# Attention steps on TensorE moved within their slots, and output-weight conversions queued behind a later Silu

## The chip, the cores and the metric

The kernel runs on one core of a Trainium2 chip. The metric is the device time of one execution in microseconds (us); a lower time is better. Chunks, blocks and slots are counted from 0 throughout.

## The reference, cut to what matters

```python
def reference(q, k, v, moe, moe2):               # q, k, v: [4, 8, 576, 64] f32
    s = q @ k.T / 8                              # per batch and head
    s = where(mask, s, -1e9)                     # heads 0-3: the last 32 keys; heads 4-7: every 32nd key
    a = exp(s - max(s)); a = a / (sum(a) + 1e-9)
    x = heads_side_by_side(a @ v)                # [2304, 512]
    xn = x / sqrt(mean(x * x) + 1e-6) * moe.rms_g
    g = xn @ moe.w_gate                          # [2304, 1536]
    y = (g / (1 + exp(-g)) * (xn @ moe.w_val)) @ moe.w_out
    return ((y @ moe2.w_a) * (y @ moe2.w_b)) @ moe2.w_out
```

## The kernel before, in words

The 2304 tokens are cut into six blocks `t` of 384. The first stage runs attention and the first expert (gate, value, output) block by block; the second stage (from some 540 us on) does the second expert and is not touched by the change. Every product is made of three matmuls, with the operands split into a rounded high part and the rest (`mm3`).

Block `t` loops over twelve chunks `fc` of 128 hidden columns. For a chunk TensorE makes `g_ps` and `v_ps` (`mm_in`, lines 485 to 488, 24 matmuls of 384 columns), VectorE scales `g_ps` by the inverse norm `rinv` into `sg` (L774), ScalarE takes the Silu of `sg` (L776), VectorE multiplies by `v_ps` (L787), ScalarE casts the result to the high part of `hl` (L506, in `split`), VectorE or GpSimd subtracts for the low part (L507), and TensorE adds the chunk into `y` (`emit_y`, 12 matmuls, one chunk behind). `g_ps` and `v_ps` share three PSUM buffers.

Woven into the chunks of block `t` is the attention of block `t + 1`. `attention_slot(steps, fc)` traces the steps of slot `fc`, after the Silu of chunk `fc` and ahead of `emit_y` of chunk `fc - 1`. The local heads' steps are placed by the strings `LOCAL` (one for block 0, one for the later blocks, slots parted by `|`): loads `ll`, `lvl`; scores `qk` on TensorE, masked on VectorE (`smask`), row maximum `lmax`, `lexp` on ScalarE, `lnorm`; transposes `pt` on TensorE (L358), copied out by ScalarE (`ptc`, L368); `pv` on TensorE (L378) and its evacuation `pvc`. The strided heads are done with products on GpSimd and sums on VectorE; at their end `xst` (L412) transposes on TensorE and `xstc` evacuates. `rms` (L444) and `rinv` (L448, L450) close a block's attention. All of the attention's TensorE results of blocks 1 to 5 go through one PSUM buffer, `att`, so `qk`, `pt`, `pv`, `xst` follow one another only after each one's evacuation. In block 0 the exponentials are grouped (`exps`): they stand behind the Silu traced last, and the next Silu stands behind them.

In block 0 the weights are converted too. Each chunk's gate and value weights (`convert1`) and output weights pass ScalarE (L137 in place, L142 into `cz`), VectorE (L145), ScalarE (L150) and a subtraction, nearly always on GpSimd (L151). `cz` has one buffer for output weights. The converted output weights `wo` are stored by SyncE's queue (L793) and read back in blocks 1 to 5 (L615). The raw output weights of chunks 8 and 9 and later of 10 and 11 share two buffers (`load_late`).

The program is traced in this order, but each engine's own order is written by a planner when the kernel is compiled (`schedule_with_timeline_sim=True`, line 1032): it goes by its own model of when an instruction has what it needs. On the chip an engine runs its list in that order. `behind(instructions)` (lines 497 to 502) tells the planner to put what is traced inside it behind the given instruction on that instruction's engine; with a Silu that is ScalarE's list alone. `gate(fc)` does the same with steps of the first block's attention.

Of the kernel before, what the change touches and what calls it, by code (L numbers as in the profile page):

```python
# [47 lines left out]
         "snorm sqr sqrt xhi",  # L48
         "rec sexp snorm sqrt xhi"]

LOCAL = [("ll0 qk0 smask0 lmax0|ll1 qk1|smask1 qk2 lmax1 smask2 lmax2||lexp0 lexp1 lexp2|"
# [3 lines left out]


STRIDED1 = ("lq ls0 ls1 sqk00 sqk01 sqk02|sqk10 sqk11 sqk12|lv0 ssub|lv1|sexp snorm|spv00 spv01 spv02|spv10 spv11|"
# [20 lines left out]
def fused_kernel(ctx: ExitStack, tc: tile.TileContext, qtl, ktl, vl, qs, ks, vs, cst, w1, w2, out):  # L78
# [7 lines left out]
    def engine(c):  # L86
        return {"P": nc.gpsimd, "D": nc.vector}[c]
# [29 lines left out]
    def load_pair(w, which, pool=None):  # L117
        if pool is None:
            t = gv_slot(U32, "gv_raw")
            if which[0][1] == 0:  # L120
                gvraw[which[0][0]] = t
            return [load_raw(w, fc, k, t[:, i]) for i, (fc, k) in enumerate(which)]
        return [load_raw(w, fc, k, raw_third(pool)) for fc, k in which]
# [46 lines left out]
    def run(steps):  # L170
        for f in steps:
            f()
# [312 lines left out]
    def mm_in(ps, w, sel, x):  # L485
        for cc in range(NCC):
            c = slice(cc * 128, (cc + 1) * 128)
            mm3(ps, w[:, sel, 0, c], w[:, sel, 1, c], x[cc][:, 0], x[cc][:, 1], cc == 0, cc == NCC - 1)

    def tmp(name):  # L490
        return act.tile([128, NTB], F32, tag="t", name=name, bufs=NTMP)

    made = []
    silu, silu_gate = [], []

    @contextmanager
    def behind(instructions):

        with ExitStack() as e:
            for i in instructions:  # L500
                e.enter_context(tc.issue_after(i))
            yield

    def split(h, lo_eng):
        hl = act.tile([128, 2, NTB], F32R, tag="hl", name="hl", bufs=3)
        made.append(nc.scalar.copy(hl[:, 0], h).ins)  # L506
        made.append(lo_eng.tensor_tensor(hl[:, 1], h, hl[:, 0].bitcast(F32), op=ALU.subtract).ins)  # L507
        return hl
# [26 lines left out]
    def load_units(n):  # L535
        for which in units[:n]:
            raw.update(zip(which, load_pair(w1, which)))
        del units[:n]

    def load_late(which):  # L540
        raw.update(zip(which, load_pair(w1, which, pool)))

    def convert1(fc):
        t = gv[fc] = gv_slot(F32R, "gv")
        two = [raw.pop((fc, k)) for k in range(2)]
        if fc in FUSEDW:
            both, ready = gvraw[fc], t.rearrange("p k a n -> p (k a) n")
            run(conversion(both.rearrange("p k a n -> p (k a) n"), ready, pool, engine(WLO[fc][0]), LOW[fc][0]))
        else:
            run(zipped(*(conversion(two[k], t[:, k], pool, engine(WLO[fc][k]), LOW[fc][k]) for k in range(2))))  # L550
# [30 lines left out]
    @contextmanager  # L581
    def gate(fc):

        with behind(silu[:1] if fc > 4 else []), ExitStack() as e:
            for key in GATES[min(fc, len(GATES) - 1)].split():
                e.enter_context(tc.issue_after(s0["st"][key].ins))
            yield
# [7 lines left out]
    def emit_y(t, fc):  # L595
        if fc == 0:
            for e in range(NCC):
                y[t, e] = psum.tile([128, 512], F32, tag=f"y{e}", name=f"y{e}")
        h = hl.pop((t, fc))
        w = wo.pop((t, fc))  # L600
        for e in range(NCC):
            c = slice(e * 128, (e + 1) * 128)
            mm3(y[t, e][:, :NTB], w[:, 0, c], w[:, 1, c], h[:, 0], h[:, 1], fc == 0, fc == NFC - 1)

    def evac_y(t):
        for e in range(NCC):
            if e % 2 == 0:
                both = act.tile([128, 2, NTB], F32, tag="x", name="ys", bufs=8)
            ys = both[:, e % 2]
            nc.vector.tensor_tensor(ys, y[t, e][:, :NTB], ri[t], op=ALU.mult)  # L610
            nc.sync.dma_start(x2d[t, e // 2][:, e % 2], ys)

    def load_wo(t, fc):
        wt = wo[t, fc] = wo_tile()
        nc.sync.dma_start(wt.rearrange("p a n -> p (a n)").bitcast(F32), wod[fc])  # L615


    local = [dict(enumerate(order.split("|"))) for order in LOCAL]
    strided1 = dict(enumerate(STRIDED1.split("|")))

    def attention_slot(steps, fc):
        st = steps["strided"]
        n_sl = 10
        if t == 0:
            part = strided1.get(fc, "").split()
        else:
            part = st[len(st) * fc // n_sl:len(st) * (fc + 1) // n_sl] if fc < n_sl else []
        part += local[min(t, 1)].get(fc, "").split()
        part += ["rms", "rinv"] * (fc == n_sl)
        for n in part:  # L630
            steps[n]()

    def exps(steps):

        def together(f, key):
            def g():
                with behind([silu[-1]]):
                    f()
                silu_gate.append(steps["st"][key].ins)
            return g  # L640

        for n in ("lexp0", "lexp1", "lexp2"):
            steps[n] = together(steps[n], "exp")
# [98 lines left out]
    for t in range(NB):  # L742
        if t == 1:
            apool.close()
            pool = apool.enter_context(tc.tile_pool(name="attn", bufs=1))
        if t == NB - 1:
            apool.close()
            cpool.close()
            pool = p2.enter_context(tc.tile_pool(name="forms", bufs=1, reuse_waits="tile"))
            early = [f for k in (4, 5, 0, 1, 2, 3) for f in convert_forms(k, k < 4)]  # L750
        nxt = attention(t + 1, pool, psum, itertools.cycle(["att"])) if t + 1 < NB else None
        if t == 0:
            exps(nxt)
        x = [xt[t, cc] for cc in range(NCC)]
        for fc in range(NFC):
            if t > 0 and fc == 0:
                load_wo(t, 0)
            g_ps = psum.tile([128, 512], F32, tag="gv", name="g_ps", bufs=3)
            mm_in(g_ps[:, :NTB], gv[fc], 0, x)
            v_ps = psum.tile([128, 512], F32, tag="gv", name="v_ps", bufs=3)  # L760
            mm_in(v_ps[:, :NTB], gv[fc], 1, x)
            if t == 0 and fc + 1 < NFC:
                with gate(fc + 1):
                    convert1(fc + 1)
                if fc + 2 == NFC:
                    load_late([(NFC - 2, 2), (NFC - 1, 2)])
            if t == NB - 1:
                slab[fc] = wgt.tile([128, 4 * DM], F32 if fc in (0, 1, 11) else F32R, tag="gv", name="slab", bufs=NFC)
                with behind(made):
                    run(early[len(early) * fc // NFC:len(early) * (fc + 1) // NFC])  # L770
                    for k in [k for k in x0 if k <= fc]:
                        run(x0.pop(k))
            sg = tmp("sg")
            nc.vector.tensor_tensor(sg, g_ps[:, :NTB], ri[t], op=ALU.mult)  # L774
            with behind(silu_gate):
                silu.append(nc.scalar.activation(sg, sg, AF.Silu).ins)  # L776
            silu_gate[:] = []
            if fc == 1 and t > 0:
                evac_y(t - 1)
            if nxt is not None:  # L780
                attention_slot(nxt, fc)
            if prev is not None:
                emit_y(*prev)
            if t > 0 and fc + 1 < NFC:
                load_wo(t, fc + 1)
            h = tmp("h") if t else v_ps[:, :NTB]
            made[:] = [nc.vector.tensor_tensor(h, sg, v_ps[:, :NTB], op=ALU.mult).ins]  # L787
            hl[t, fc] = split(h, engine(HLO0[fc] if t == 0 else HLO[t]))
            if t == 0:
                wt = wo[0, fc] = wo_tile()  # L790
                with gate(fc + 1), behind(silu[:1] if fc > 1 else []):
                    run(conversion(raw.pop((fc, 2)), wt, pool, engine(WLO[fc][2]), LOW[fc][2], True))
                nc.sync.dma_start(wod[fc], wt.rearrange("p a n -> p (a n)").bitcast(F32))  # L793
                if fc % 2 and units:
                    load_units(1)
            prev = (t, fc)
    emit_y(*prev)
    evac_y(NB - 1)
# [138 lines left out]
    steps = [(ps, g, p) for ps in (range(0, 3), range(3, 6)) for g in range(NB // 2) for p in ps]  # L937
# [99 lines left out]
```

## Time and profile before

| | |
|---|---|
| time, median of 3 runs (lowest, highest) | 965.81 us (964.63, 966.51) |
| the profiled execution: time, span of the trace | 967.4 us, 965.6 us |
| mean granted TensorE clock in the span | 0.985 |
| busy share of the span: TensorE matmuls, VectorE, ScalarE, GpSimd | 97%, 64%, 44%, 56% |
| block 0 with its attention and conversions | from 33 to some 133 us |

The 1.8 us between the profiled time and its span lie outside the first and last instruction. A busy time of TensorE counts overlapping matmuls, so the steps between starts, the waits and the granted clock tell more than the share does.

### The profile page before, as it was taken

What the parts mean: (1) busy time and instruction counts of PE and PEld (TensorE: products, weight loads), DVE (VectorE), ACT (ScalarE), POOL (GpSimd) and SP (SyncE); (2) the same over time, 40 slices, a digit from 0 to 9 for tenths busy, and PEclk for the clock granted to TensorE, in tenths of its full rate; (3) what the DMA queues carried; (4) which work ended last, traced back from release to release, by engine and by line L of the source; (5) the groups of instructions that cost most, each with busy time, mean ns of one, the idle gap of its engine ahead of it and who ended that gap; (6) DMA issues with size and microseconds to landing.
All of it is one profiled execution on the core that took longest, in us unless ns stands there. A gap on an engine that the chain in (4) does not pass through costs nothing.

```text
span 965.6 us, 14099 instructions
## 1 busy us (share of the span) xinstructions
PE 937.1 (97%) x5318; PEld 888.2 (92%) x5318; DVE 621.5 (64%) x900; ACT 425.3 (44%) x795; POOL 539.5 (56%) x407
## 2 busy tenths in 40 slices
PE   5998999999999999999999899999999999999998
PEld 4898999999999999999999898899999998999996
DVE  5658858658819895986666378658655655564534
ACT  5988646344433434434555455436425422122110
POOL 3567946558649677878479545655724423123211
PEclk6899999999999999999999999999999999999999
DMA  9974286537535563532788884996993974754701
GB/s 342 408 262 151 89 288 218 151 96 225 165 104 161 161 204 102 185 105 87 284 324 306 329 306 166 402 415 247 385 373 114 345 274 165 284 205 168 267 2 66
DMA packets 57363, 215.55 MB, mean 223 GB/s; under 512 B 5968, under 2 KB 14544, under 8 KB 51664
## 3 DMA queue, kind: packets, MB, share of 16 engines
q1 hardware_dynamic: 57296, 214.66, 61.3%
q8 instruction: 42, 0.69, 0.3%
q14 instruction: 25, 0.20, 0.1%
HBM read 172.17 MB, written 42.47 MB: 222 GB/s over the span
## 4 chain that ended last, share of the span: by engine, by line
PE 65%; DMA 11%; DVE 7%; POOL 7%; ACT 4%; issue 4%; SPq 0%; DVEq 0%; ACTq 0%; POOLq 0%
PE o L916 5%; PE o L918 5%; PE o L917 5%; DMA raw<-in_w 4%; POOL prod L248 4%; PE Y L862 4%; PE Y L861 4%; PE Y L860 4%; DMA gv_raw<-in_w 3%; PE y L482 3%; PE y L481 3%; PE g_ps L483 3%; PE y L483 3%; PE g_ps L482 3%; PE g_ps L481 3%
## 5 line engine op out<-in xcount | busy, mean ns | idle before, releaser
L151 POOL TENSOR_TENSOR hl<-c,hl 128x384 fp32r<-128x384 f32 x72 | 77.9, 1082 | 181.0 <-ACT hl L150 174.4
L248 POOL TENSOR_TENSOR prod<-kv_t,qs_t 128x512 f32<-128x512 f32 (+12 forms) x57 | 108.3, 1921 | 15.3 <-DMA kv_t<-in_ks 8.2
L481 PE MATMUL v_ps<-xx,gv 128*128 128x384 f32 x288 | 97.7, 339 | 1.9 <-DVE sg L774 1.8
L482 PE MATMUL y<-hl,wo 128*128 128x384 f32 x288 | 98.1, 341 | 1.1 <-POOL hl L507 1.1
L281 POOL TENSOR_TENSOR prod<-kv_t,S_t 128x512 f32<-128x512 f32 (+12 forms) x57 | 86.2, 1526 | 21.1 <-issue 7.1
L482 PE MATMUL v_ps<-xx,gv 128*128 128x384 f32 x288 | 97.9, 340 | 0.0
L483 PE MATMUL v_ps<-xx,gv 128*128 128x384 f32 x288 | 97.8, 340 | 0.0
L481 PE MATMUL g_ps<-xx,gv 128*128 128x384 f32 x288 | 97.5, 339 | 0.0
L483 PE MATMUL g_ps<-xx,gv 128*128 128x384 f32 x288 | 97.3, 338 | 0.0
L482 PE MATMUL g_ps<-xx,gv 128*128 128x384 f32 x288 | 96.9, 337 | 0.0
L867 DVE TENSOR_TENSOR c<-c,Y 128x384 f32<-128x384 f32 x108 | 59.0, 551 | 58.8 <-PE Y L862 53.5
L507 POOL TENSOR_TENSOR hl<-h,hl 128x384 fp32r<-128x384 f32 x60 | 64.1, 1069 | 58.4 <-ACT hl L506 57.3
L483 PE MATMUL y<-hl,wo 128*128 128x384 f32 x288 | 95.0, 338 | 0.0
L284 DVE TENSOR_REDUCE xs_t<-prod 128x64 f32<-128x448 f32 (+17 forms) x57 | 85.7, 1521 | 9.7 <-POOL prod L281 9.5
L481 PE MATMUL y<-hl,wo 128*128 128x384 f32 x288 | 85.0, 343 | 7.0 <-ACT hl L506 5.4
L916 PE MATMUL o<-slab,hl 128*128 128x512 f32 x216 | 84.7, 393 | 1.8 <-DVE slab L925 1.3
L917 PE MATMUL o<-slab,hl 128*128 128x512 f32 x216 | 84.5, 392 | 0.0
L918 PE MATMUL o<-slab,hl 128*128 128x512 f32 x216 | 83.2, 394 | 0.0
L150 ACT CAST hl<-c 128x384 fp32r<-128x384 f32 x72 | 37.0, 514 | 93.8 <-DVE c L897 93.5
L776 ACT ACTIVATE sg<-sg 128x384 f32<-128x384 f32 x72 | 38.0, 528 | 86.4 <-DVE sg L774 86.0
L862 PE MATMUL Y<-slab,form 128*128 128x384 f32 x216 | 73.0, 338 | 0.0
L861 PE MATMUL Y<-slab,form 128*128 128x384 f32 x216 | 73.0, 338 | 0.0
(137 smaller groups left out, 2491.4 us busy)
## 6 DMA issues: line engine op xcount, KB each, us to landing
form<-formd SPq DMA_DIRECT2D x32, 1792.0 KB, 10.7
wo<-wod SPq DMA_DIRECT2D x60, 512.0 KB, 3.8
raw<-in_w SPq DMA_DIRECT2D x40, 512.0 KB, 7.3
gv_raw<-in_w SPq DMA_DIRECT2D x32, 512.0 KB, 10.2
formd<-form SPq DMA_DIRECT2D x6, 1792.0 KB, 7.5
formd<-forms SPq DMA_DIRECT2D x6, 1792.0 KB, 12.8
slab<-x2d SPq DMA_DIRECT2D x24, 384.0 KB, 4.0
wod<-wo SPq DMA_DIRECT2D x12, 512.0 KB, 3.4
```

What stands on the lines that cost most here:

```text
L151: lo_eng.tensor_tensor(lo, x, hi.bitcast(F32), op=ALU.subtract)
L248: nc.gpsimd.tensor_tensor(pr, st["ks", g][:, :, :n, :], st["qs"][:, heads(g), mm:mm + 1, :].to_broadcast([128, G, n, D]), op=ALU.mult)
L281: st["pvm"] = nc.gpsimd.tensor_tensor(pr, st["vs", g][:, :, :n, :], st["S"][:, heads(g), mm, :n, None].to_broadcast([128, G, n, D]), op=AL ...
L284: st["pvr"] = nc.vector.tensor_reduce(st["xs"][:, mm, heads(g), :], pr.rearrange("p g n d -> p g d n"), axis=X, op=ALU.add)
L481: nc.tensor.matmul(out_ps, w_hi, x_hi, start=start, stop=False)
L482: nc.tensor.matmul(out_ps, w_hi, x_lo, start=False, stop=False)
L483: nc.tensor.matmul(out_ps, w_lo, x_hi, start=False, stop=stop)
L861: nc.tensor.matmul(bank(n), hi, x[p][:, 1, c], start=False, stop=False, skip_group_check=not begins)
L862: nc.tensor.matmul(bank(n), lo, x[p][:, 0, c], start=False, stop=c == 1, skip_group_check=not begins)
L916: nc.tensor.matmul(o, h[:, 0, cols], w[0], start=n == 0, stop=False)
L917: nc.tensor.matmul(o, h[:, 0, cols], w[1], start=False, stop=False)
L918: nc.tensor.matmul(o, h[:, 1, cols], w[0], start=False, stop=n == len(chunks) - 1)
```

## The change

Three things are done. The strings `LOCAL` place the local heads' steps anew: in block 0 `pt`, `pv` and their copies come later by up to one slot; in blocks 1 to 4 the local loads come a slot earlier, the three `lexp` stand together in slot 3, and `pt0` moves from slot 4 to 5. A `/` in a slot parts steps that are traced where the slot was from steps that are traced behind the chunk's `emit_y`, `split` and, in block 0, output-weight conversion; `xst1` and `xstc1` always go to that second place. And the output-weight conversion of chunk `n` (from 2 on) is put behind the Silu of chunk `n - 2`, where it stood behind the Silu of chunk 0.

```diff
-LOCAL = [("ll0 qk0 smask0 lmax0|ll1 qk1|smask1 qk2 lmax1 smask2 lmax2||lexp0 lexp1 lexp2|"
-          "lnorm0 lvl0 pt0 ptc0 lnorm1 lvl1|pt1 ptc1 lnorm2 pt2 ptc2|pv0 pvc0 pv1 pvc1||"),
-         ("|ll0 qk0|ll1 qk1 smask0 smask1 qk2 lmax0 lmax1|lvl0 smask2 lexp0 lmax2 lexp2|"
-          "lnorm0 lexp1 lvl1 pt0 ptc0 lnorm1 lnorm2|pt1 pt2 ptc1||ptc2 pv0 pvc0 pv1 pvc1||")]
+LOCAL = [("ll0 qk0 smask0 lmax0|ll1 qk1 smask1 lmax1|qk2 smask2 lmax2||lexp0 lexp1 lexp2|"
+          "lnorm0 lvl0 lnorm1 lvl1 lnorm2|pt0 ptc0/pt1 ptc1|pt2 ptc2|pv0 pvc0/pv1 pvc1||"),
+         ("ll0|qk0 smask0 lmax0 ll1|qk1 smask1 lmax1/qk2 smask2 lmax2|lexp0 lexp1 lexp2 lvl0|"
+          "lnorm0 lnorm1 lnorm2 lvl1|pt0 ptc0/pt1 ptc1|pt2 ptc2|pv0 pvc0/pv1 pvc1||")]
...
-    def attention_slot(steps, fc):
+    def attention_slot(steps, fc, late):
...
-        part += local[min(t, 1)].get(fc, "").split()
-        part += ["rms", "rinv"] * (fc == n_sl)
+        part = [n for n in part if (n in ("xst1", "xstc1")) == late]
+        early, _, behind_y = local[min(t, 1)].get(fc, "").partition("/")
+        part += (behind_y if late else early).split()
+        part += ["rms", "rinv"] * (fc == n_sl and not late)
...
             if nxt is not None:
-                attention_slot(nxt, fc)
+                attention_slot(nxt, fc, False)
             if prev is not None:
                 emit_y(*prev)
...
-                with gate(fc + 1), behind(silu[:1] if fc > 1 else []):
+                with gate(fc + 1), behind(silu[max(fc - 2, 0):max(fc - 1, 1)] if fc > 1 else []):
                     run(conversion(raw.pop((fc, 2)), wt, pool, engine(WLO[fc][2]), LOW[fc][2], True))
...
+            if nxt is not None:
+                attention_slot(nxt, fc, True)
             prev = (t, fc)
```

## Rows read from the trace of the kernel before

**Rows 1.** The page: an engine's busy us (share) and count; a load's KB, landing us.

```profile
PE 937.1 (97%) x5318; PEld 888.2 (92%) x5318; DVE 621.5 (64%) x900; ACT 425.3 (44%) x795; POOL 539.5 (56%) x407
...
wo<-wod SPq DMA_DIRECT2D x60, 512.0 KB, 3.8
```

**Rows 2.** Windows: stretch, length, busy PE, PEld, DVE, ACT, POOL, granted clock, DMA share.

```profile
33.00:60.00 27.00, 23.54 (x123) 21.97 (x122) 16.31 (x20) 26.67 (x40) 10.14 (x5) 0.94 1.03 408
60.00:86.00 26.00, 26.00 (x168) 25.61 (x166) 19.19 (x31) 20.47 (x51) 24.27 (x14) 1.00 0.37 124
86.00:96.00 10.00, 6.99 (x32) 5.84 (x31) 9.59 (x15) 9.45 (x17) 4.43 (x3) 0.83 0.57 197
96.00:133.00 37.00, 35.62 (x225) 34.07 (x225) 28.79 (x35) 25.94 (x43) 26.14 (x17) 1.00 0.38 133
...
134.00:540.00 406.00, 403.40 (x2467) 393.72 (x2466) 280.98 (x377) 177.63 (x341) 292.75 (x216) 1.00 0.57 190
```

**Rows 3.** TensorE's waits, 34 to 134 us: total us, times, longest.

```profile
PE y L481 <- ACT hl L506: 5.4, 3, 2.1
```

**Rows 4.** TensorE's timeline at chunk 0's output: start, us, instruction, idle time before it.

```profile
49.59 0.34 PE L483 MATMUL v_ps<-xx,gv 128*128 128x384 f32 x1
51.78 0.97 PE L481 MATMUL y<-hl,wo 128*128 128x384 f32 x4 [1.85 <-ACT hl L506]
```

**Rows 5.** The chain that ended last, from 51 us: start, us, what.

```profile
51.37 0.36 ACT hl L506
...
53.29 0.32 PE y L483
...
56.49 0.27 PE g_ps L483
...
57.10 0.18 PE g_ps L483
...
64.58 0.88 PE att L296 x8
```

**Rows 6.** ScalarE's timeline, 45 to 59 us.

```profile
45.09 0.67 ACT L137 ACTIVATE gv_raw<-gv_raw 128x512 f32<-128x512 f32 x1
...
46.20 2.80 ACT L137 ACTIVATE gv_raw<-gv_raw 128x512 f32<-128x512 f32 x4
48.87 0.55 ACT L776 ACTIVATE sg<-sg 128x384 f32<-128x384 f32 x1
...
51.23 0.50 ACT L506 CAST hl<-v_ps 128x384 fp32r<-128x384 f32 x1
...
53.14 1.30 ACT L137 ACTIVATE gv_raw<-gv_raw 128x512 f32<-128x512 f32 x2
...
58.21 0.73 ACT L137 ACTIVATE raw<-raw 128x512 f32<-128x512 f32 x1
```

**Rows 7.** VectorE's timeline: the scaled gate of chunk 1.

```profile
46.96 0.56 DVE L774 TENSOR_TENSOR sg<-g_ps,rinv 128x384 f32<-128x384 f32 x1
```

**Rows 8.** TensorE's timeline, 87 to 90 us.

```profile
87.01 0.61 PE L358 MATMUL att<-cst_sb,s_t 128*96 128x128 f32 x4 [0.71 <-ACT pt L368]
89.75 0.96 PE L481 MATMUL y<-hl,wo 128*128 128x384 f32 x4 [2.13 <-ACT hl L506]
```

**Rows 9.** Timelines at the end of block 0, on TensorE, ScalarE and VectorE.

```profile
119.03 0.27 PE L412 MATMUL att<-cst_sb,xs_t 128*128 128x128 f32 x1
...
123.54 0.67 ACT L137 ACTIVATE raw<-raw 128x512 f32<-128x512 f32 x1 [0.40 <-DMA raw<-in_w]
...
124.37 0.81 PE L444 MATMUL att<-sq,ones 128*128 128x384 f32 x2
...
128.09 0.58 ACT L448 ACTIVATE rms_t<-att,eps_sb 128x384 f32<-128x384 f32 x1
...
128.71 2.55 DVE L450 RECIPROCAL rinv<-rms_t 128x384 f32<-128x384 f32 x1 [0.74 <-ACT rms_t L448]
...
132.83 0.96 PE L481 MATMUL y<-hl,wo 128*128 128x384 f32 x4 [1.39 <-ACT hl L506]
```

## The prediction

> **What bounds the kernel now.** I read the page's busy shares first [rows 1]: TensorE is at 97%, no other engine over 64%, so a change that adds or drops no matmul can win only where TensorE waits or runs at its lower clock. The table of windows then says where that is [rows 2]. From 134 to 540 us, which are blocks 1 to 5, TensorE is busy 403.40 of 406 at a clock of 1.00: at most 2.6 us lie there for the taking. From 60 to 86 it is busy throughout. What is left stands in block 0: 3.46 idle us from 33 to 60 (clock 0.94), 3.01 from 86 to 96 (clock 0.83) and 1.38 from 96 to 133. The view of waits gives most of it one name: in that block TensorE waited three times, 5.4 us in all, for ScalarE's cast of `hl` [rows 3]. The three waits are 1.85 at 51.78 [rows 4], 2.13 at 89.75 [rows 8] and 1.39 at 132.83 [rows 9].
>
> The first one is where the third edit strikes. `hl` of chunk 0 is cast at 51.23, behind the Silu of chunk 1 at 48.87, and straight ahead of that Silu stand four L137 [rows 6]; ScalarE is busy 26.67 of 27 us in this stretch [rows 2]. Three of the four have the form of output weights, by the order of the loads those of chunks 3, 4 and 5; the fourth prepares a chunk's gate and value weights. Nobody needs the three soon: the matmuls that read them are three chunks and more away. The chain that ended last goes through just this cast: from `hl` at 51.37 to TensorE, which then runs without a wait until the first scores at 64.58 [rows 5], and over VectorE and GpSimd to the end of block 0. So a cast that comes earlier is worth something beyond its own gap. TensorE's clock falls right behind the wait: the matmuls from 53.29 to 56.49 advance by 0.32 us each, those from 57.10 on by 0.18 [rows 5]. That is 1.2 GHz against 2.4 GHz, after TensorE had been idle for 1.85 us.
>
> **The change, part by part.** The sum is made against the profiled execution (967.4 us, span 965.6, 1.8 outside it); it lies 1.6 us over the median of 965.81, and I take the gain off that median.
>
> *Conversions behind Silu n-2.* The edit acts on ScalarE's list alone. The steps of chunk n that stand ahead of Silu n-2 today are L137: three ahead of Silu 1 at 48.87, two at 53.14 (chunks 6 and 7) and two up to 58.21 (chunks 8 and 9) [rows 6]. Their later steps need the one `cz` buffer and come behind their Silu already. One L137 of this form takes 0.67 and, overlapping the next, moves the list on by about 0.56 (at 46.20 four, one of them of the double form, take 2.80) [rows 6]. Without three of them Silu 1 could start 1.68 earlier, at 47.19; but its input is ready at 47.52 [rows 7], so it starts at about 47.57 and the gain is 1.30. The cast moves from 51.23 to 49.93, and `y`, which started 0.55 behind it, to 50.48. TensorE is free at 49.93 [rows 4]. The wait of 1.85 becomes 0.55: **1.30 us gained**. Bounds: 0, if the planner puts other ready work in the freed places, or L137 of chunk 3, free behind Silu 1, ahead of the cast together with it; 1.85, if the cast is planned before the gate weights that stand between it and Silu 1.
>
> *The clock behind that wait.* Eleven matmuls, from the one at 53.29 to the one at 56.49, at 0.32 instead of 0.18 cost 11 x 0.14, some **1.55 us** [rows 5]. With the idle time cut to less than a third I take the fall as gone; bounds 0 and 1.55. The Trainium skill, "TensorE: Matmul & The Clock Gate", section "Seeing it yourself", warns that the clock events of a trace have been seen to be unreliable. If the fall were a fault of the record, this term would be nothing and the forecast 964.9. The start steps of 0.32 and 0.18 are not clock events, and they show the fall as well, so I keep the term.
>
> *The L137 that move.* Those of chunks 3 to 6 go to places between 48.87 and some 66, ScalarE has 5.5 idle us from 60 to 86 [rows 2]: nothing. Those of chunks 7 to 9 now stand behind Silu 5, 6 and 7. The cast of chunk 5, which can't come before Silu 5, is the one that TensorE waits for until 89.75 [rows 8], so these three land in the stretch from 86 to 96, where ScalarE is busy 9.45 of 10 [rows 2]. Ahead of that cast they would cost up to 1.68; they are traced later than it and I take 0. VectorE's, GpSimd's and SyncE's steps of the conversions follow; the stores of `wo` are first read back at the start of block 1, and a load of it lands after 3.8 us [rows 1].
>
> *`pt1`, `pt2` behind `y`.* TensorE now does `pt1` at 87.01 inside its hole, after 0.71 of waiting for the copy of `pt0`, and then waits for the cast of chunk 5 until 89.75 [rows 8]. Behind `y` of chunk 5 the hole goes from 86.3 to 89.75 as before, since the cast of chunk 5 is what ends it, and the four transposes come on top: a loss of **0.4** (0.61 as the row has them, less their overlap with what follows; bounds 0 and 0.61). The stall that the edit is meant for isn't removed, it changes its name.
>
> *`pv1`, `xst1`, `xstc1` later.* They are all links of one chain over the single `att` buffer. `xst1` ends today at 119.03, when its last input comes, the sum of squares is added up by 124.37, and the root of it follows only at 128.09, behind other work on ScalarE [rows 9]: between the end of that matmul (125.2) and the root lie some 2.9 us in which the chain may slip. One output group of 12 matmuls is 2.1 us. I take 0; the bound is 5 us of slip less that slack, see the rivals.
>
> *Blocks 1 to 5.* There are at most 2.6 idle us, and no wait of weight for attention. The same slips against the same kind of slack apply. The loads `ll0` and `ll1`, a slot earlier on SyncE's queue, stand ahead of the loads of `wo` of chunk 1 and later; these land in 3.8 us [rows 1], and a chunk takes 36 matmuls at 0.18, 6.3 us, so there is cover of 2.5. I take 0; bounds: 1.4 gained, 2 lost.
>
> Sum: 1.30 + 1.55 - 0.4 = 2.45 gained. The profiled execution would be 964.95, the median **963.4**. For this the second gap at 89.75 and the one at 132.83 keep their size, and everything from 51 on comes earlier, as the chain of waits suggests.
>
> **The rivals.** *The far end holds.* The end of block 0 may be set by something else than TensorE's start at 51: the output weights of chunks 10 and 11 wait for a raw buffer (the data of chunk 11 are touched at 123.54, straight as they land), pass one `cz` buffer, and `rinv` is ready at 131.26 [rows 9]. If these don't come earlier, TensorE arrives early and the wait of 1.39 at 132.83 grows by what was won. Against it: GpSimd, which carries this end, starts its dense stretch behind 60 (24.27 of 26 busy, after 10.14 of 27) [rows 2], when ScalarE's casts come, and these come earlier too. Gain 0 to 1.3, time 964.5 to 965.8; the same time results if the change doesn't do what it says because the planner fills ScalarE's freed places with other conversions. Together 0.28.
>
> *The attention chain becomes the bound* (slower). `pt1` behind `y` of chunk 5 ends at 92.3 rather than 87.6, a slip of 4.7; if `pt2`, `pv0`, `pv1` and `xst` pass this on link by link, each behind another output group, `rinv` of block 1 slips by 4.7 - 2.9 = 1.8 for the first link and by up to 2.1 for each of two further groups, 6 in all. It decides as soon as the slip exceeds those 2.9. `rinv` frees the three PSUM buffers of the next block, so TensorE stops for it. Price 1.8 to 6 against 2.45 won: 965.2 to 969.4, in the middle 967.5; a longer stop can also lower the clock once more. For it: the buffer is single, and the planner orders by priority. Against it: the exponentials hold `pt` up more than its slot does. 0.22.
>
> *The second hole closes too.* If the earlier front brings the exponentials and so the cast of chunk 5 ahead of TensorE, 0.71 + 2.13 and the lower clock from 86 to 96 (0.83 of 10 us, some 1.6) go as well: 4.4 more, 959.0. ScalarE and VectorE stand at 95% there [rows 2], which speaks against it: 0.07.
>
> **How the numbers follow.** The forecast (2.45, from some 1.6 to 3.2) has 0.43. A measurement of this kernel can tell about 0.2% from no change, 1.9 us. Of the forecast's 0.43 about 0.33 lie beyond that; with 0.07 of the second hole and a little of the first rival's edge, faster 0.44. Within 0.2%: 0.10 of the forecast, nearly all of 0.28, and the lower edge of the slower rival, 0.35. Slower: 0.21. The likeliest case alone gives 962.6 to 964.2; the range goes to 960.0 and 968.5, which leaves out most of the second hole's case and the slower rival's upper quarter.
>
> **What would show it.** Right: in ScalarE's list before Silu 1 only the gate weights' L137 is left, the cast of chunk 0 comes near 49.9, TensorE's wait there is about 0.5 and no steps of 0.32 follow; `pt1` stands behind `y` of chunk 5, and the hole there is one wait for the cast; the end of block 0 comes about 2.5 earlier. Wrong: the cast stays near 51.2 with other work ahead of it; or it moves and the wait at the end of block 0 grows by as much; or `rms` and `rinv` come later than 124.4 and 131.3 and TensorE waits at the start of block 1 or of a later block. What would make the prediction wrong above all is the planner, which orders all engines anew from its own model: a move in block 0 that none of the edits names.

## The result, and the profile after

The changed kernel takes 972.43 us (971.38 to 972.70, four runs) against 965.73 (964.63 to 966.51, four runs): a ratio of 1.0068, 95% interval 1.0056 to 1.0080. It is slower by 6.7 us, where 2.4 us of gain were forecast, and it lies above the range (960.0 to 968.5). The profiled execution took 972.65 us, its span is 970.9, 5.3 longer than that of before.

TensorE's waits after the change, 34 to 134 us and 134 to 540 us (total us, times, longest):

```profile
PE v_ps L481 <- DVE sg L776: 9.1, 3, 6.2
PE g_ps L481 <- DVE sg L776: 1.3, 1, 1.3
PE y L481 <- ACT wo L150: 0.2, 1, 0.2
...
PE y L482 <- POOL hl L507: 1.6, 3, 0.9
PE att L296 <- DVE s_t L314: 1.2, 1, 1.2
PE v_ps L481 <- DVE sg L776: 0.5, 1, 0.5
PE y L481 <- ACT hl L506: 0.2, 1, 0.2
```

The waits for the cast of `hl` in block 0, 5.4 us before [rows 3], are gone. In their place TensorE waits for VectorE's scaled gate `sg`, which frees the PSUM buffer that the next `v_ps` needs (L776 is the L774 of before, L778 the Silu of L776, L789 the product of L787). In the first stretch the waits listed rise from 7.9 (5.4, 1.8 for `sg`, 0.7 for `pt`) to 10.6, in the second from 1.4 to 3.5: 4.8 us more. The windows of after have the columns of [rows 2]:

```profile
86.00:96.00 10.00, 3.79 (x16) 3.47 (x15) 6.93 (x12) 9.93 (x15) 4.11 (x3) 0.76 0.13 52
96.00:133.00 37.00, 36.83 (x228) 34.74 (x227) 27.22 (x34) 26.19 (x46) 25.11 (x17) 0.97 0.42 147
...
134.00:540.00 406.00, 402.48 (x2461) 392.68 (x2460) 282.03 (x379) 179.84 (x342) 288.69 (x209) 1.00 0.55 185
```

From 86 to 96 TensorE is busy 3.79 us of ten where it was busy 6.99 [rows 2], with ScalarE at 9.93. The clock is at 1.2 GHz for some 7 us around and behind the hole (0.24 of 10 us and 0.03 of 37 are missing, at half speed), where it was 3.4 [rows 2]; but TensorE stands idle in the first 2.4 of them, so the lower clock costs only some 0.5 more than before. 4.8 and 0.5 add up to the 5.3 of the span. That they meet to the tenth is luck: from 134 to 540 the windows show only 0.9 us more of idle time (2.6 before [rows 2], 3.5 after), where the listed waits grow by 2.1.

Most of the loss is one hole. With a wait of 1.33 for `sg` just ahead of it, at 84.91, TensorE stands still for 7.5 us there, where it stood still for 3.0 before (0.71 and 2.13 [rows 8], and 0.16 for `sg`). The front and the end of block 0 give 1.8 of that back. The timeline of TensorE, ScalarE and VectorE at the hole:

```profile
93.46 0.69 PE L481 MATMUL v_ps<-xx,gv 128*128 128x384 f32 x1 [6.21 <-DVE sg L776]
...
86.77 0.53 ACT L778 ACTIVATE sg<-sg 128x384 f32<-128x384 f32 x1
87.20 1.66 ACT L137 ACTIVATE gv_raw<-gv_raw 128x512 f32<-128x512 f32 x2
88.88 1.28 ACT L264 ACT_TABLE_LOAD   x1
90.17 0.26 ACT L264 ACTIVATE S_t<-S_t 128x72 f32<-128x72 f32 x1
90.45 1.28 ACT L778 ACT_TABLE_LOAD   x1
91.75 0.52 ACT L778 ACTIVATE sg<-sg 128x384 f32<-128x384 f32 x1
...
92.30 0.56 DVE L789 TENSOR_TENSOR v_ps<-sg,v_ps 128x384 f32<-128x384 f32 x1 [1.40 <-ACT sg L778]
92.91 0.50 DVE L776 TENSOR_TENSOR sg<-g_ps,rinv 128x384 f32<-128x384 f32 x1
```

Read it from the end. TensorE waits for `sg` of chunk 7 at 92.91; that stands on VectorE's list behind `h` of chunk 6 at 92.30, which waits for Silu 6 at 91.75. (Before, VectorE made these two the other way round, `sg` at 90.29 and `h` at 90.75. The attention edits alone turn them round too, and lose nothing.) Between Silu 5 and Silu 6 lie two L137 (1.66), and the exponential of the strided scores (L264) with a table load on either side: 1.28 + 0.26 + 1.28. Of the two L137 only the first, 0.65 long, is an output-weight conversion that the third edit moved. The other has the form of a chunk's gate and value weights, and one of that form stood between these two Silus before as well. The second L137 alone, in a narrower view of after, and ScalarE before, from Silu 5 to the cast of chunk 5:

```profile
87.76 1.10 ACT L137 ACTIVATE gv_raw<-gv_raw 128x1024 f32<-128x1024 f32 x1
```

```profile
85.87 0.53 ACT L776 ACTIVATE sg<-sg 128x384 f32<-128x384 f32 x1
...
87.82 1.12 ACT L137 ACTIVATE gv_raw<-gv_raw 128x1024 f32<-128x1024 f32 x1
88.83 0.51 ACT L776 ACTIVATE sg<-sg 128x384 f32<-128x384 f32 x1
89.25 0.45 ACT L506 CAST hl<-v_ps 128x384 fp32r<-128x384 f32 x1
```

In the kernel before, this exponential stood behind Silu 7, at 93.86. No edit of the diff names it. Its input was ready sooner after the change: GpSimd's last product for the strided scores (L248) ended at 80.6 instead of 85.1. That the planner moved it for this reason is argued; its model is not on record.

### The profile page after: what moved, and what is told of

Its sections match the earlier page's. It is cut to its first block, busy times and chain, and to the rows that moved or that the text cites. A ratio compares the mean times of both kernels' runs of the same rounds, so it can differ in the third digit from the quotient of the medians.

```text
span 970.9 us, 14096 instructions
## 1 busy us (share of the span) xinstructions
PE 938.2 (97%) x5318; PEld 889.2 (92%) x5318; DVE 620.2 (64%) x900; ACT 427.9 (44%) x797; POOL 541.5 (56%) x407
## 4 chain that ended last, share of the span: by engine, by line
PE 70%; DVE 7%; POOL 7%; ACT 6%; DMA 5%; issue 4%; SPq 1%; POOLq 0%; DVEq 0%; ACTq 0%
PE o L920 5%; PE o L922 5%; PE o L921 5%; PE Y L866 4%; PE Y L864 4%; PE Y L865 4%; PE y L482 3%; PE y L481 3%; PE v_ps L483 3%; PE v_ps L481 3%; PE y L483 3%; PE g_ps L481 3%; PE g_ps L483 3%; PE v_ps L482 3%; PE g_ps L482 3%
## 5 line engine op out<-in xcount | busy, mean ns | idle before, releaser
L248 POOL TENSOR_TENSOR prod<-kv_t,qs_t 128x512 f32<-128x512 f32 (+12 forms) x57 | 106.8, 1898 | 23.6 <-DMA kv_t<-in_ks 12.8
L150 ACT CAST hl<-c 128x384 fp32r<-128x384 f32 x72 | 36.9, 513 | 93.8 <-DVE c L901 93.5
L778 ACT ACTIVATE sg<-sg 128x384 f32<-128x384 f32 x72 | 37.8, 525 | 80.5 <-DVE sg L776 80.0
## 6 DMA issues: line engine op xcount, KB each, us to landing
form<-formd SPq DMA_DIRECT2D x32, 1792.0 KB, 10.6
```

What stands on the lines that cost most here:

```text
L248: nc.gpsimd.tensor_tensor(pr, st["ks", g][:, :, :n, :], st["qs"][:, heads(g), mm:mm + 1, :].to_broadcast([128, G, n, D]), op=ALU.mult)
```

## The experiments

Medians and 95% intervals are against the kernel before, timed beside each group of runs (965.50 to 965.91).

**The change taken apart.** Three runs: the third edit alone, the attention edits alone, and the attention edits in blocks 1 to 4 alone.

```diff
+ with gate(fc + 1), behind(silu[max(fc - 2, 0):max(fc - 1, 1)] if fc > 1 else []):   # first run: this alone
...
+ LOCAL, attention_slot(steps, fc, late)    # second run: these alone; third: only where t > 0
```

> The kernel before with the third edit alone: output-weight conversion n behind Silu n-2, the attention steps where they were. Theory A (the Exp of the strided heads comes between two Silus of block 0): with fewer L137 at the front the strided scores are ready earlier, the planner then puts that Exp (L264) between Silu 5 and Silu 6, which costs two table loads of 1.28 us on ScalarE, and TensorE waits some 6 us for the scaled gate of chunk 7 near 87 and then runs some 7 us at 1.2 GHz. It expects the greater part of the loss here: 968.5 to 971. Theory B (the moved attention steps do it: transposes behind the output group, one PSUM buffer): expects no loss here, 963 to 966.

> The changed kernel with the conversions behind Silu 0 again, so the attention edits alone. Theory A: the Exp stands behind Silu 7 as before the change, no long wait near 87; 965 to 968, of which up to 2 in block 1. Theory B: the long wait near 87 to 93 is here, 969 to 972.

> Conversions and block 0's attention as before the change; only the attention steps woven into blocks 1 to 4 are placed as changed. In the changed kernel's trace TensorE waits 1.2 us for the masked scores near 156 and 1.0 near 180, which the kernel before doesn't have. If these belong to the placement: 966.5 to 968. If they are a consequence of what block 0 leaves: 965.2 to 966.2.

Measured: 974.96 us, ratio 1.0082 (1.0058 to 1.0105), for the conversions alone; 966.55, 1.0007 (0.9996 to 1.0017), for the attention edits alone; 966.46, 1.0007 (0.9997 to 1.0016), in the later blocks alone. The third edit carries the whole loss. Alone it takes even 2.5 us more than the changed kernel (the intervals overlap), above the 968.5 to 971 that I expected, and not by the hole that I expected: TensorE's longest wait is 3.81, for the copy of `pt` behind the exponential, and its listed waits from 134 to 540 are 5.4 us where they were 1.4. Why blocks 1 to 5 lose so much there stays open. The attention edits can't be told from no change, so the slower rival that I had written down, the attention chain, falls. (Their trace does have a long wait near 87, of 3.62 for the copy of `pt`, where I expected none; 3.0 us of waits stood there before.) The later blocks alone end between my two cases and decide nothing by their time.

**The exponential tied to the local ones**, so that it shares their table and needs no loads of its own:

```diff
+        steps["sexp"] = together(steps["sexp"], "sexp")
```

> The changed kernel, with the strided Exp of block 1's attention put into the group of exponentials that stands behind Silu 4 and ahead of Silu 5, so that no table load of its own is needed. Theory A: two table loads of 1.28 us fall away behind Silu 5, the wait near 87 shrinks from 6.2 to 2 to 4 us and the low clock behind it with it; 965 to 968.5. Theory B: the wait stays where the transposes and the casts are, 970 to 973.

Measured: 970.74, ratio 1.0040 (1.0028 to 1.0053), and a hole of 3.72 where it was 6.21: the wait of theory A, with a time in theory B's range. The table loads are part of the loss, 1.7 of 6.7 us; a new wait of 2.3 for `wo` at 114 takes some back.

**Which conversions.** The third edit for chunks 2 to 5 alone, and for chunks 6 to 9 alone (10 and 11 with them; the rest as before):

```diff
+ behind(silu[fc - 2:fc - 1] if 1 < fc < 6 else silu[:1] if fc > 1 else [])   # first chunks
+ behind(silu[fc - 2:fc - 1] if fc >= 6 else silu[:1] if fc > 1 else [])      # last chunks
```

> The kernel before, with only the conversions of chunks 2 to 5 put behind the Silu two chunks earlier; chunks 6 to 9 stay behind the first Silu, and the attention slots are those of before. What differs: three conversions leave the front of Silu 1, none is brought into the stretch from 86 to 96 us. Theory A (the relief at the front lets GpSimd's strided products end some 4 us earlier, and the planner then puts their exponential and its table load between two late Silus): the exponential stands between Silu 6 and Silu 7, TensorE waits 2 to 6 us between 86 and 98 at v_ps or att, and the time is 970 to 975. Theory C (the conversions of chunks 6 to 9, which leave the place behind the first Silus and come to stand behind Silu 4 to 7, are the cause): nothing is lost here, the waits from 86 to 96 are those of before (0.7 and 2.1) and the time is 963 to 967, by some 0.65 below before if the gain at the front stays.

> The kernel before, with only the conversions of chunks 6 to 9 put behind the Silu two chunks earlier; chunks 2 to 5 stay behind the first Silu, and the attention slots are those of before. What differs: the front of Silu 1 is as crowded as before, but two to four conversions leave the places behind Silu 1 (53 to 58 us) and come to stand behind Silu 4 to 7. Theory A (the relief ahead of Silu 1 is the cause): the wait of 1.85 at 50 us stays as before, and so does all behind it, 965 to 967. Theory C (these conversions are the cause, by standing in ScalarE's full stretch and by letting the strided exponential in between Silu 5 and Silu 6): TensorE waits 4 to 6 us in one hole between 86 and 98, at half clock behind it, and the time is 970 to 975.

Measured: 967.32, ratio 1.0014 (1.0004 to 1.0023), for the first chunks; 970.73, 1.0050 (1.0033 to 1.0067), for the last. Theory A falls: relieving ScalarE ahead of Silu 1 isn't the cause of the greater part. Its signs did come with the first chunks, an exponential between Silu 6 and 7 (at 90.31) and a wait of 3.20 at `v_ps` (until 88.25), but this wait ends before the exponential's table load, and the run loses only 1.4 us. The last chunks are the cause, with the front as it was. TensorE's and ScalarE's timelines of that run (its profiled execution took 968.74):

```profile
86.54 0.61 PE L358 MATMUL att<-cst_sb,s_t 128*96 128x128 f32 x4 [2.21 <-ACT pt L368]
91.79 1.65 PE L481 MATMUL y<-hl,wo 128*128 128x384 f32 x4 [4.64 <-ACT hl L506]
...
84.27 1.66 ACT L137 ACTIVATE gv_raw<-gv_raw 128x512 f32<-128x512 f32 x2
85.82 0.57 ACT L368 COPY pt<-att 96x512 f32<-96x512 f32 x1
86.41 1.28 ACT L264 ACT_TABLE_LOAD   x1
87.70 0.26 ACT L264 ACTIVATE S_t<-S_t 128x72 f32<-128x72 f32 x1
87.87 1.11 ACT L142 ACTIVATE cz<-gv_raw 128x1024 uint32<-128x1024 uint16 x1
89.00 1.28 ACT L776 ACT_TABLE_LOAD   x1
90.30 0.52 ACT L776 ACTIVATE sg<-sg 128x384 f32<-128x384 f32 x1
90.73 0.65 ACT L137 ACTIVATE raw<-raw 128x512 f32<-128x512 f32 x1
91.28 0.46 ACT L506 CAST hl<-v_ps 128x384 fp32r<-128x384 f32 x1
```

Two L137, the moved one of 0.64 and the gate weights' one, now stand ahead of the copy of `pt` (wait 2.21 where it was 0.71), then the table loads, a further L137 that moved, and only then the cast of chunk 5, which ended a wait of 2.13 before [rows 8]. From Silu 5 to this cast ScalarE takes 7.44 us where it took 3.38: 2.8 of the difference are the exponential and its loads, 1.1 the two moved L137 (0.56 each, as the prediction has it). How the exponential got there shows on GpSimd's timeline, first before, then in this run:

```profile
60.74 4.76 POOL L151 TENSOR_TENSOR gv<-cz,gv 128x1024 fp32r<-128x1024 f32 x2 [6.68 <-DMA gv_raw<-in_w]
83.25 1.85 POOL L248 TENSOR_TENSOR prod<-kv_t,qs_t 128x768 f32<-128x768 f32 x1
```

```profile
57.49 4.77 POOL L151 TENSOR_TENSOR gv<-cz,gv 128x1024 fp32r<-128x1024 f32 x2 [4.51 <-ACT gv L150]
73.28 4.38 POOL L248 TENSOR_TENSOR prod<-kv_t,qs_t 128x640 f32<-128x640 f32 x2
```

With the L137 of chunks 6 to 9 gone from 53 to 58 us, ScalarE's cast of the gate weights (L150) and GpSimd's subtraction behind it come 3.3 us sooner, and the products end at 77.7 instead of 85.1. (About 1.1 of both differences is not the edit's: at 50.68, with the same order on ScalarE, `y` of chunk 0 is already that much earlier than before.) With the first chunks alone the subtraction starts at 60.11 and the exponential stands behind Silu 6. The eleven traces in which nothing holds the exponential agree on the order: where VectorE takes the row maximum of these scores (L260) at 80.4 to 83.4, it stands between Silu 5 and 6; at 85.8 to 86.7, between 6 and 7; at 88.0 to 90.2, behind 7.

**How much is the exponential, how much the conversions.** The last chunks with the exponential tied as above; and the exponential held behind Silu 7, in the changed kernel and in the run with the last chunks:

```diff
-            "... |lv0 ssub|lv1|sexp snorm|spv00 spv01 spv02|spv10 spv11|spv12||xst0 xstc0 xst1 xstc1")
+            "... |lv0 ssub|lv1||||sexp snorm|spv00 spv01 spv02 spv10 spv11 spv12|xst0 xstc0 xst1 xstc1")
...
+                with behind([silu[-1]]):    # around sexp
+                    f()
```

> The run with the conversions of chunks 6 to 9 moved, plus one thing: the exponential of the strided scores is tied to the exponentials of the local ones, so that it takes no table loads of its own between Silu 5 and Silu 6. Same four conversions in the same places of the Silus. Theory C1 (the loss is the two table loads and the exponential between these Silus, 1.28 + 0.27 + 1.28 = 2.8 us): the wait of 4.64 at y of chunk 5 falls to about 1.8 and the time goes to within 2 us of before, 965 to 968. Theory C2 (the loss is the raw conversions in front of Silu 6 and of the cast, 0.65 and 1.66 us, and the two table loads only use what they left): the hole stays above 3 us and the time at 969 to 972.

> The changed kernel with one thing held back: the exponential of the strided scores is ordered behind Silu 7, where it stands in the kernel before, instead of between Silu 5 and Silu 6; the four steps behind it follow one to three slots later. The conversions of chunks 6 to 9 stay where the change puts them. Theory C1 (the loss is the exponential with its two table loads ahead of Silu 6, 2.8 us): the wait of 6.2 at v_ps of chunk 7 falls to 3.5 or less, nothing of that size takes its place, and the time is 967 to 969.5. Theory C2 (the conversions that now stand ahead of Silu 6 and of the casts carry it): a hole of 5 us or more between 84 and 98 stays, 970 to 973.

> The run with only the conversions of chunks 6 to 9 moved, with the exponential of the strided scores held behind Silu 7 in the same way. The front is that of before and the attention slots too, but for the steps behind the exponential. Theory C1: the waits of 2.21 and 4.64 between 84 and 92 shrink to those of before (0.7 and 2.1) within 1 us, and the time is 965 to 967.5. Theory C2: 4.5 us or more of waits stay there and the time is 969 to 972.

Measured: 967.79, ratio 1.0024 (1.0014 to 1.0035), for the tied one, 2.9 us less than without the tie and C1's time, though not by C1's path: its profile (of an execution of 969.88) has one hole of 5.03 at `v_ps`. Held behind Silu 7, the changed kernel takes 970.10, 1.0036 (1.0024 to 1.0047), and the run with the last chunks 969.66, 1.0036 (1.0025 to 1.0048), both in C2's range. In the changed kernel the hole halves, as C1 has it, but a new wait opens at the end of block 0:

```profile
89.51 0.56 PE L481 MATMUL v_ps<-xx,gv 128*128 128x384 f32 x1 [3.13 <-DVE sg L784]
...
134.13 0.69 PE L481 MATMUL g_ps<-xx,gv 128*128 128x384 f32 x1 [2.37 <-DVE sg L784]
```

In the second run 6.85 us of waits (2.21, 4.64) become 3.90 (2.23, 1.67), between the two theories, and 2.19 appear at the same place of the end:

```profile
87.47 0.61 PE L358 MATMUL att<-cst_sb,s_t 128*96 128x128 f32 x4 [2.23 <-ACT pt L368]
89.75 1.33 PE L481 MATMUL y<-hl,wo 128*128 128x384 f32 x4 [1.67 <-ACT hl L506]
```

Part of these 2.19 may be my own doing: the steps behind the exponential came one to three slots later, and the root for block 1's `rinv` starts at 129.21 instead of 128.09 [rows 9], with `y` of chunk 5 at 89.75 in both. So both causes are real, and these traces give their shares of the hole. Of the 4.0 us by which the last chunks lengthen the two waits (6.85 for 2.84), 2.95 go with the exponential and its loads, and the 1.06 that stay are the two moved L137. In the changed kernel 3.1 of the hole's 6.21 go with the exponential. The expectations above count 1.66 for the L137, with the gate weights' one, which isn't new. In time the shares don't show: held late, the exponential gives back 2.3 us in the changed kernel and 1.1 in the other, where the intervals overlap. It can stand neither early (Silu 6 pays) nor as late as I put it (the end of block 0 pays).

**The changed kernel without the last chunks:** its attention slots, chunks 2 to 5 moved, 6 to 11 as before.

> The changed kernel with all of its attention slots, and with its conversions of chunks 2 to 5 behind Silu n-2, but those of chunks 6 to 9 behind the first Silu as before. If the conversions of chunks 6 to 9 carry the loss whatever the attention slots are, the wait of 6.2 at v_ps of chunk 7 is gone, no hole between 84 and 98 us is above 3.5, and the time is that of the run with the first chunks only, 966 to 968.5. If loss needs the attention slots and the front relief together, it stays at 970 to 973.

Measured: 968.12, ratio 1.0029 (1.0019 to 1.0039), with a wait of 3.18 at 88. That is 4.3 us below the changed kernel: the last chunks carry two thirds of the loss with the attention slots, too.

**The front's term by itself.** The kernel before with the conversion of chunk 5 alone behind Silu 3:

```diff
+ behind(silu[fc - 2:fc - 1] if fc == 5 else silu[:1] if fc > 1 else [])
```

> The kernel before with one conversion moved, that of chunk 5, from the front to behind Silu 3. One of the three conversions leaves the list ahead of Silu 1, and VectorE still scales the gate of chunk 2 before it makes h of chunk 1, unlike with three. The term of my sum for the front, taken in its smallest form: the cast of chunk 0 comes 0.56 earlier and the wait of 1.85 at 51.8 becomes 1.3. If that is worth anything at the far end the time is 964 to 965.4; if the rest of block 0 takes it back, it is that of before within 0.1%, 965 to 966.9; if every move of these conversions costs something later, over 967.

Measured: 967.65, ratio 1.0018 (1.0010 to 1.0027). The timelines of TensorE and ScalarE:

```profile
50.60 0.98 PE L481 MATMUL y<-hl,wo 128*128 128x384 f32 x4 [1.07 <-ACT hl L506]
88.05 0.92 PE L358 MATMUL att<-cst_sb,s_t 128*96 128x128 f32 x4 [4.23 <-ACT pt L368]
132.57 0.96 PE L481 MATMUL y<-hl,wo 128*128 128x384 f32 x4 [1.80 <-ACT hl L506]
...
87.33 0.57 ACT L368 COPY pt<-att 96x512 f32<-96x512 f32 x1
```

The front does what the sum says, and a little more: the wait of 1.85 is 1.07, and no fall of the clock follows. And nothing comes of it: the run is 1.8 us slower than the kernel before, the last of my three cases. TensorE reaches the second hole earlier, but the copy of `pt` that ends it, on a ScalarE with no pause from 83 on, comes at 87.33, and the hole is 4.23 + 0.45 where it was 0.71 + 2.13 + 0.16. The gain at the front is waited away 35 us later, and more than the gain.

**Does the far end hold it?** The same kernel, and the kernel before, with the load of chunk 11's output weights left out (chunk 11 is converted from the buffer of chunk 9):

```diff
-                    load_late([(NFC - 2, 2), (NFC - 1, 2)])
+                    load_late([(NFC - 2, 2)])
+                    raw[NFC - 1, 2] = raw_9
```

> The run with the one conversion of chunk 5 moved, and the load of chunk 11's output weights left out: chunk 11 is converted from what stands in the buffer of chunk 9, so its values are not those of the reference. The front's gain of some 2 us stays to 83 us in that run and is gone at the end of block 0, whose chain goes through the load of chunk 11 (3.48 us from 119.75, behind VectorE's step on chunk 9 that frees the buffer) to the wait of 1.80 at y of chunk 11. Theory F (the far end, by this load, takes the front's gain): the wait of 1.80 at 132 falls below 0.6 and the time by 1.2 to 2, to 965.6 to 966.5, while the same omission in the kernel before gives no more than 1.4. Theory G (the gain is lost in the hole at 88 already, 4.2 us there against 3.0, and nothing is left to hold): the wait at 132 shrinks, but the difference between this run and the kernel before without that load stays at or above 1.5.

> The kernel before with the load of chunk 11's output weights left out in the same way (chunk 11 is converted from the buffer of chunk 9). It prices the far end alone: if the load of 3.49 us at 120.03 sets the wait of 1.39 at y of chunk 11, that wait goes and the time is 964.2 to 965.2; if rinv of block 1 or ScalarE's queue holds the same point anyway, the wait stays above 0.8 and the time is 965.3 to 966.5.

Measured: 966.59, ratio 1.0011 (1.0002 to 1.0020), and 965.39, 0.9999 (0.9990 to 1.0008). Without the load the kernel before is no faster, and its last wait is 1.16 for 1.39. Theory F falls: with the load gone the wait at the end is still 1.57, not under 0.6. G's number isn't met either, since the two runs differ by 1.2 us where it asked for 1.5 or more; but its hole is there, 4.22 + 0.32 at 88. That the gain is lost at 88 us is so read from the traces, and no run removes that hole to show it. What does set the wait at the end of block 0 stays open. No version here is faster than the kernel before.

## Why the prediction was wrong

**The step that failed** is the third term, "The L137 that move": taken as 0, with a bound of 1.68. Moving those of chunks 6 to 9 (and 10 and 11 with them) costs 4.8 us alone. I had seen that these conversions land in the stretch where ScalarE is busy 9.45 of 10 [rows 2], and took nothing because they are traced behind the cast. Yet in that run the planner put one ahead of the copy of `pt` and one ahead of the cast, 1.1 us of the 4.0 by which the hole grew, within my bound. The rest had no price at all. I counted what the conversions bring where they go, not what they free where they leave: with the room at 53 to 58 GpSimd's products ended 4.5 us sooner in the changed kernel and 7.4 with the last chunks alone, and an exponential and two table loads, 2.8 us, came into that same stretch. That was the danger of the prediction's last lines, "a move in block 0 that none of the edits names"; it had no price and no share of the range.

**Conversions behind Silu n-2 (1.30 gained).** The cast of chunk 0 came at 50.38, near the 49.93 of the sum, and `y` still started later, at 52.22 for 51.78 [rows 4]. The waiting place had moved, as the lines of after show. The line ahead of them is VectorE's before the change:

```profile
41.89 1.01 DVE L774 TENSOR_TENSOR sg<-g_ps,rinv 128x384 f32<-128x384 f32 x2
```

```profile
47.45 0.52 ACT L778 ACTIVATE sg<-sg 128x384 f32<-128x384 f32 x1
48.00 0.56 DVE L789 TENSOR_TENSOR v_ps<-sg,v_ps 128x384 f32<-128x384 f32 x1 [0.75 <-ACT sg L778]
48.47 0.55 DVE L776 TENSOR_TENSOR sg<-g_ps,rinv 128x384 f32<-128x384 f32 x1
49.08 0.44 PE L481 MATMUL v_ps<-xx,gv 128*128 128x384 f32 x1 [1.94 <-DVE sg L776]
```

I read the L774 at 46.96 [rows 7] as the input of Silu 1. It is the scaled gate of chunk 2: those of chunks 0 and 1 stand together at 41.89, so Silu 1's input was ready long before, and Silu 1 starts at 47.45 here, ahead of the 47.52 that I held to be its bound. With Silu 1 earlier, `h` of chunk 1 is ready earlier and the planner puts it ahead of that scaled gate, whose PSUM buffer TensorE needs. Two waits, 0.65 at 47.57 and 1.85, became one of 1.94; `y` of chunk 1 starts 0.65 earlier than before (57.01 for 57.66), half of the term; behind the hole nothing of it is left. Where one conversion leaves instead of three, the order stays and the term is right in size (0.78 measured, 0.56 expected).

**The clock behind the wait (1.55).** Not gone in the changed kernel, since a wait of 1.94 stands at its place; gone behind the wait of 1.07. It isn't a fixed property of the kernel before either (last section).

**`pt1`, `pt2` behind `y` (0.4 lost), `pv1` and `xst1` later (0), blocks 1 to 5 (0)**: the attention edits alone give 0.07%, within their interval of nothing. These terms were right as far as a measurement can tell. In the changed kernel block 1 has a wait of 1.2 for L314 that the later blocks' edits alone don't show, and the run with the last chunks alone has one of 0.7: it follows from block 0. The chain did slip in the changed kernel: the sum of squares is at 131.15 for 124.37 [rows 9], and the root follows straight behind it, at 132.01, so the slack of 2.9 is used up. But no wait of TensorE stands between 116 and 156.

**The rivals.** "The far end holds" was right that a gain at the front is lost later, in the run that makes one, and had the wrong place, as far as the traces show: the second hole, not the last load. "The second hole closes too" went the other way: it is the hole that grew. The range left out the case that came, because I gave the planner's own moves no price.

## What to carry to other kernels

Where a planner writes the order, price a moved step at both ends: what it delays where it lands, and what it lets in where it leaves, down to the next change of activation table. A gain ahead of a stretch in which another engine runs without a pause is worth what that engine gains, not what the waiting one does; look for the next hole before adding it to a sum. And tell an operation's chunk by who reads it, not by its place in the timeline.

## What the runs showed of the hardware

**The clock falls behind a wait in one execution and not in another.** ScalarE's order up to the cast of chunk 0 is the same in seven of these kernels. Before, TensorE waited 1.85 there [rows 4] and the clock fell [rows 5]. With the attention edits alone, the timeline and the window from 50 to 60 us:

```profile
51.25 0.98 PE L481 MATMUL y<-hl,wo 128*128 128x384 f32 x4 [1.58 <-ACT hl L506]
...
50.00:60.00 10.00, 8.75 (x50) 8.75 (x51) 6.28 (x9) 10.00 (x16) 3.54 (x2) 1.00 1.04 408
```

The clock (third column from the right) stayed at 2.4 GHz there, as it did behind 1.64, 1.65 and 1.68 (last chunks, no last load, last chunks with the late exponential); it fell to 1.2 behind 1.79 and 1.83 (later blocks alone, last chunks with the tied exponential). The length of a wait alone doesn't decide it: in the run with the first chunks the clock stayed at 2.4 GHz behind a wait of 3.20 at 88.25. The three executions with the fall differ from the other four before it already: TensorE's wait for `sg` at 42 is 0.95 or 0.96 in them and 1.13 to 1.22 in the four. What sets that stays open. The runs of one kernel differ in the same way: of the ten with the later blocks alone, four have a mean granted clock of 0.985 and spans of 965.2 to 965.6, five have 0.989 and 963.5 to 964.5. So 1.6 us of a single profile can belong to the execution and not to the edit.

**The same small operation takes far longer beside other work.** VectorE's L346, on 128 x 4 and 64 x 8 values, before and after:

```profile
77.95 0.16 DVE L346 TENSOR_SCALAR lsm<-lsm 128x4 f32<-128x4 f32 x1
...
84.59 0.54 DVE L346 TENSOR_SCALAR lsm<-lsm 64x8 f32<-64x8 f32 x1 [1.86 <-ACT s_t L336]
```

```profile
85.49 2.32 DVE L346 TENSOR_SCALAR lsm<-lsm 64x8 f32<-64x8 f32 x1 [0.73 <-ACT s_t L336]
...
85.39 2.40 POOL L151 TENSOR_TENSOR gv<-cz,gv 128x1024 fp32r<-128x1024 f32 x1
```

After, it ends with GpSimd's subtraction of weights, within 0.02 us; the run with the last chunks has the same pair (2.32 from 82.56, 2.40 from 82.46). Before, it ends within 0.03 us of GpSimd's product that starts at 83.25, shown above, so its 0.54 holds a wait too. At 77.95, when GpSimd pauses between two products (77.88 to 78.11), it takes 0.16. The Trainium skill, "SBUF — State Buffer", section "SBUF: two separate sides", says that VectorE and GpSimd share a pair of ports which the one that starts first keeps for its whole instruction, while the other blocks; it says so of VectorE operations in a two-port mode or with two inputs in SBUF. The common ends agree with that. Which mode L346 runs in no row shows, and no run takes the subtraction away, so that the ports are the cause is argued, not shown.
